# An attention and two-MoE kernel on one core: q and k by block transposes, w_in split on chip, expert weights in 6 KB pieces

## Chip, cores and metric

The program runs on one core of a Trainium2 chip. The metric is the device time of one execution in microseconds, the median of several runs; lower is better. An execution with a profile beside it gives the trace from which all rows below come.

## The reference

Three stages follow each other; everything is float32 at the interface (w_in and w_out arrive as 64-bit floats).

```
attention: q, k, v (4 batches, 12 heads, 448 x 64), causal softmax      -> x (1792 x 768)
MoE 1:     h = x @ w_in (768 x 2048); g = h * clip(h + 3, 0, 6) / 6; x2 = g @ w_out
MoE 2:     logits = x2 @ phi (768 x 32); softmax over tokens -> slot_input = d.T @ x2 (32 x 768)
           per expert e of 8, 4 slots each: relu(slot_input[e] @ w1[e]) @ w2[e]
           out = softmax over slots(logits) @ slot_out                 (1792 x 768)
```

w1 is 8 x 768 x 1024 and w2 8 x 1024 x 768, 25.2 MB each; the output is 5.5 MB.

## The kernel before

**A planner writes the program.** The function records steps (an engine or a choice of engines, a supposed cost, the steps it depends on, the buffers it uses, a priority). `Schedule.run` then picks steps one after the other by its own clock and emits them; each engine executes its instructions in that order. The table `TU` (L20) holds the priorities of the stages, biases and buffer counts. All DMAs are issued from SP, in one order, on one queue of 16 DMA engines; a DMA whose buffer isn't free holds up those behind it.

**Attention** (L408) works on pairs of heads, six pairs per batch, 24 in all. For q and for k of a pair, `ld` (L416) loads both heads to a tile of 112 partitions in pieces of 256 bytes; `tr` (L431) makes four PE transposes into PSUM; ACT copies the result to the rounded half `qp[:,0]` or `kp[:,0]`; DVE subtracts to get the rest, `[:,1]` (L440). Then come the scores for the maxima (L457, DVE L472), the maxima's diagonal (L486 to L490, on POOL or DVE), the scores again, transposed (L507, L512), exp on ACT (L522), the causal cut on POOL (L530), the product with v (L545), normalisation on DVE and a transpose back (L566).

**w_out and w_in** are converted from 64-bit floats once (`conv`, L581: raw load of 768 KB, ACT, three DVE steps). w_out goes to a scratch `wo_d` in DRAM. w_in, in 16 parts `ft` of 128 columns, is split into a rounded half (ACT, L682) and a rest (DVE L685 or POOL L687), in the tile `wpl` of 768 KB. In batch 0 the converted part is stored to `wf_d` (384 KB) and the split pair to `wi_d` (768 KB). Batches 1 and 2 load the split pair straight from `wi_d`. Batch 3 loads the 384 KB from `wf_d` and splits again. There are two `wpl` and two `cx` buffers.

**MoE 1** (`hmm`, L698 to L701) takes 18 matmuls for each `ft`, 64 such groups in all, called H0 to H63 here. Its activation (L706, L708), the transposes of g (L715) and the logits (L730) follow each. Groups of batch b stand between the attention pairs of batch b+1, so that PE has both at hand.

**MoE 2** waits for the whole of MoE 1. It loads w1 as 32 tiles of 768 KB in pieces of 2 KB (L1015), and w2 in three column chunks of 384, 256 and 128 (`DCH`, L881): 16 tiles of 768 KB in pieces of 1.5 KB, 16 of 512 KB in pieces of 1 KB, 8 of 512 KB in pieces of 512 bytes. The tiles, `ring`, become free as earlier stages release memory: twelve of w1 are loaded before H63 ends. Each chunk of w2 ends with a short chain: copy (L1133), a PE sum over row groups (L1138), ACT and DVE (L1140, L1142), 16 products (L1155 and its copies L1164, L1168) and four output DMAs. The first chunk's outputs are issued among the later loads.

## Time and profile before

| What | Value |
|---|---|
| median of 3 runs | 681.69 us (681.17 to 682.29) |
| profiled execution, own time | 680.19 us |
| its span, first to last instruction | 678.4 us |
| PE busy | 628.4 us (93%) |
| DVE, ACT, POOL busy | 329.7, 261.4, 96.5 us |
| DMA | 161.56 MB, 238 GB/s over the span |
| packets | 142615, of which 71632 under 512 B |

The profile counts busy time per engine, cuts the span into slices, follows the chain of waits back from the end, and gives for any stretch the busy time of each engine, the clock granted to PE, and how much of the DMA engines' time was taken. A DMA share slightly over 1 means that packets overlap on an engine.

### The profile page before, as it was taken

What the parts mean: (1) busy time and instruction counts of PE and PEld (TensorE: products, weight loads), DVE (VectorE), ACT (ScalarE), POOL (GpSimd) and SP (SyncE); (2) the same over time, 40 slices, a digit from 0 to 9 for tenths busy, and PEclk for the clock granted to TensorE, in tenths of its full rate; (3) what the DMA queues carried; (4) which work ended last, traced back from release to release, by engine and by line L of the source; (5) the groups of instructions that cost most, each with busy time, mean ns of one, the idle gap of its engine ahead of it and who ended that gap; (6) DMA issues with size and microseconds to landing.
All of it is one profiled execution on the core that took longest, in us unless ns stands there. A gap on an engine that the chain in (4) does not pass through costs nothing.

```text
span 678.4 us, 15815 instructions
## 1 busy us (share of the span) xinstructions
PE 628.4 (93%) x6556; PEld 478.2 (70%) x6556; DVE 329.7 (49%) x814; ACT 261.4 (39%) x488; POOL 96.5 (14%) x197
## 2 busy tenths in 40 slices
PE   8798989999999999999999999999999999977474
PEld 6677868787888778888888688888698843522133
DVE  6886978888784534444335554323433333101101
ACT  2575566544544433323334332334344322201011
POOL 1332332325340011110001001000000000000000
PEclk7998999999999999999999999999999999996666
DMA  8989899989979833555445343335962399999997
GB/s 205 312 293 297 270 262 335 338 236 333 298 267 361 264 89 122 157 159 138 141 142 168 91 135 124 124 135 212 370 239 93 117 341 385 378 373 357 331 313 220
DMA packets 142615, 161.56 MB, mean 238 GB/s; under 512 B 71632, under 2 KB 113872, under 8 KB 142544
## 3 DMA queue, kind: packets, MB, share of 16 engines
q1 hardware_dynamic: 142544, 160.56, 72.9%
q8 instruction: 51, 0.84, 0.5%
q14 instruction: 20, 0.16, 0.1%
HBM read 129.86 MB, written 30.67 MB: 237 GB/s over the span
## 4 chain that ended last, share of the span: by engine, by line
PE 68%; DMA 13%; DVE 9%; SPq 3%; issue 2%; ACT 2%; POOL 0%; DVEq 0%; ACTq 0%; POOLq 0%
PE ph L701 19%; PE pl L701 13%; DMA ring<-in_moe_w_dram 7%; PE ps L507 5%; PE t L715 5%; DVE ps L472 4%; DMA raw<-in_moe_w_out_dram 3%; PE o L545 3%; SPq L401 3%; PE t L566 3%; PE ps L457 2%; PE t L434 2%; PE t L859 2%; PE ps L1025 2%; PE ph L730 2%
## 5 line engine op out<-in xcount | busy, mean ns | idle before, releaser
L701 PE MATMUL ph<-xp,wpl 128*128 128x448 f32 x720 | 157.0, 371 | 0.0
L701 PEld LDWEIGHTS ph<-xp,wpl 128*128 128x128 f32 x720 | 132.2, 188 | 15.2 <-ACT r L706 2.2
L701 PE MATMUL pl<-xp,wpl 128*128 128x448 f32 x432 | 94.2, 371 | 0.0
L701 PEld LDWEIGHTS pl<-xp,wpl 128*128 128x128 f32 x432 | 79.4, 188 | 9.0 <-issue 2.6
L472 DVE CUSTOM_DVE_ANT_0 ps<-ps,maskw 128x448 f32<-128x448 f32 (+3 forms) x144 | 61.7, 429 | 48.5 <-PE ps L457 38.6
L530 POOL TENSOR_SCALAR_AFFINE_SELECT s<-s 128x256 f32<-128x256 f32 x96 | 43.6, 478 | 232.9 <-ACT s L522 141.5
L706 ACT ACTIVATE r<-ph,three 128x448 f32<-128x448 f32 x40 | 25.5, 637 | 102.5 <-PE ph L701 102.5
L507 PE MATMUL ps<-qp,kp 64*64 64x64 f32 (+3 forms) x576 | 57.5, 306 | 3.8 <-ACT s L522 3.8
L522 ACT ACTIVATE s<-ps 128x896 f32<-128x896 f32 (+2 forms) x72 | 50.3, 734 | 25.9 <-PE ps L512 22.0
L708 DVE SCALAR_TENSOR_TENSOR g<-r,ph 128x448 f32<-128x448 f32 x40 | 24.7, 618 | 62.9 <-ACT r L706 62.9
L507 PEld LDWEIGHTS ps<-qp,kp 64*128 64x128 f32 (+1 forms) x576 | 42.1, 175 | 17.7 <-issue 6.6
L545 PE MATMUL o<-vr,s 128*64 128x65 f32 (+1 forms) x1536 | 53.6, 224 | 0.0
L545 PEld LDWEIGHTS o<-vr,s 128*64 128x64 f32 (+1 forms) x1536 | 48.6, 137 | 5.8 <-issue 3.8
L587 ACT ACTIVATE ca<-raw 128x768 f32<-128x768 f32 x32 | 29.3, 917 | 29.7 <-DMA raw<-in_moe_w_out_dram 10.0
L708 DVE SCALAR_TENSOR_TENSOR g<-r,pl 128x448 f32<-128x448 f32 x24 | 14.8, 617 | 50.8 <-ACT r L706 50.8
L720 ACT ACTIVATE gtok<-t 128x384 f32<-128x384 f32 x64 | 31.2, 487 | 19.2 <-PE t L715 19.0
L715 PE MATMUL t<-ident,g 128*128 128x128 f32 (+1 forms) x256 | 37.9, 279 | 0.2 <-DVE g L708 0.2
L706 ACT ACTIVATE r<-pl,three 128x448 f32<-128x448 f32 x24 | 15.3, 636 | 58.3 <-PE pl L701 58.3
L596 DVE SCALAR_TENSOR_TENSOR cw<-ca,cw 128x768 uint32<-128x768 uint32 x32 | 32.9, 1029 | 3.4 <-ACT ca L587 1.7
L1123 PE MATMUL o<-ring,wos 128*32 128x384 f32 (+1 forms) x256 | 22.5, 474 | 11.8 <-DMA ring<-in_moe_w_dram 11.8
L715 PEld LDWEIGHTS t<-ident,g 128*128 128x128 f32 (+1 forms) x256 | 26.9, 133 | 6.1 <-issue 1.5
L457 PE MATMUL ps<-kp,qp 64*128 64x448 f32 (+1 forms) x192 | 27.3, 344 | 4.1 <-DVE mc L472 3.0
(209 smaller groups left out, 827.1 us busy)
## 6 DMA issues: line engine op xcount, KB each, us to landing
ring<-in_moe_w_dram SPq DMA_DIRECT2D x45, 768.0 KB, 11.6
wpl<-wi_d SPq DMA_DIRECT2D x32, 768.0 KB, 4.2
raw<-in_moe_w_out_dram SPq DMA_DIRECT2D x16, 768.0 KB, 6.1
raw<-in_moe_w_in_dram SPq DMA_DIRECT2D x16, 768.0 KB, 7.4
wi_d<-wpl SPq DMA_DIRECT2D x16, 768.0 KB, 6.1
ring<-in_moe_w_dram SPq DMA_DIRECT2D x21, 512.0 KB, 8.0
wo_d<-gtok SPq DMA_DIRECT2D x16, 384.0 KB, 4.1
wf_d<-cx SPq DMA_DIRECT2D x16, 384.0 KB, 7.5
```

The costliest lines, as they stand in the source:

```text
L457: nc.tensor.matmul(ps.t[:n, h, c:c + w], pl["q"].t[r, 0, q0:q0 + n], pl["k"].t[r, 0, 0:w], start=(t == part[0][0]), stop=adds, skip_group_ ...
L472: nc.vector.tensor_tensor_reduce(out=x, in0=x, in1=maskw[:n, 320 - q0:320 + n] if t else maskw[:n, 320:320 + n], scale=-1.0, scalar=3.0e38 ...
L507: nc.tensor.matmul(ps.t[:kn, h, col:col + n], pl["k"].t[r, x, q0:q0 + kn], pl["q"].t[r, y, q0:S], start=(c == 0 and col == 0), stop=False, ...
L522: nc.scalar.activation(out=o, in_=x, func=ACTF.Exp, scale=SCALE)
L530: nc.gpsimd.affine_select(out=x, in_=x, pattern=[[0, 2], [1, kn]], compare_op=ALU.is_ge, fill=0.0, base=0, channel_multiplier=-1)
L545: nc.tensor.matmul(o.t[64 * h:64 * h + 64, VD * j:VD * j + VD], s.t[:kn, h, c:c + 64], vr.t[:kn, h, t, :], start=(t == 0), stop=(t == ts[- ...
L596: e = sc.add("DVE", 1.04, lambda: nc.vector.scalar_tensor_tensor(out=cw.t, in0=ca.t.bitcast(U32), scalar=3, in1=cw.t, op0=ALU.logical_shif ...
L701: nc.tensor.matmul(h.t[:, :S], w.t[:, a, kk, :], x.t[:, c, kk, :], start=(n == 0), stop=(n == len(seq) - 1))
L706: rr = sc.add("ACT", 0.63, lambda h=h, r=r: nc.scalar.activation(out=r.t, in_=h.t[:, :S], func=ACTF.Relu, bias=three), [hh], [h, r], pr - ...
L708: gg = sc.add("DVE", 0.62, lambda h=h, r=r, g=g: nc.vector.scalar_tensor_tensor(out=g.t, in0=r.t, scalar=6.0, in1=h.t[:, :S], op0=ALU.min, ...
L715: nc.tensor.transpose(tp.t[:n, t * P:(t + 1) * P], g.t[:, t0:t0 + n], ident)
L720: nc.scalar.activation(out=gflat[:, :3 * DFF].rearrange("p (t f) -> p t f", f=DFF)[:, :, c], in_=v3[:, 0:3, :], func=ACTF.Copy)
```

## The change

Four things, and a new table of planner numbers.

1. For batches 1 to 3 (pairs 6 to 23, `DV`), q and k are loaded in 32 x 32 blocks, pieces of 128 bytes, four DMAs a tensor instead of two. DVE transposes the blocks in one instruction into an SBUF tile `tt` of which there are two; ACT and DVE (or POOL) split from there.
2. w_in's split is never stored. Batch 0 stores the converted part (384 KB); batches 1 to 3 load it and split it on ACT and DVE or POOL.
3. w1 is read as 32 tiles of 768 KB in contiguous pieces of 6 KB. w2 of experts 0 to 5 likewise (24 tiles, both column halves); w2 of experts 6 and 7 in two column halves (8 tiles, pieces of 1.5 KB). Rows of a weight matrix thus lie on partitions in another order, and two small operands (`sis`, `hs`) are read by PE with a stride to match.
4. The output comes in two column halves of 384 instead of three chunks; all eight output DMAs stand behind the last weight load. Both halves are summed in one PSUM tile.

```diff
-TU = {'PO': [0.0, -20.32, -45.9, 12.37], 'TO': [5.04, -0.39, 13.98, 19.64], 'PB': 0.45, 'AB': 0.24, 'TB': 274.35, 'DUTY': 0.6, 'RINGS': [2, 4, 2, 3, 1, 6, 2, 3], 'LOOK': 0.44, 'FILL': 0.96, 'RAW': 3, 'CA': 1, 'CW': 1, 'S': 2, 'PAIR': 15.98, 'UNIT': 2.62, 'WP0': 17.76, 'WPS': 10.66, 'T0': 138.06, 'L0': 10.86, 'L1': 6.43, 'GP': 217.47, 'TP': 6.75, 'ZP': 84.29, 'UP': -2.56, 'P0': 12.1, 'NQ': 2, 'WAIT': 0.12, 'AHEAD': 2.2, 'LAT': 0.23, 'CX': 2, 'G': 5, 'R': 1, 'VR': 2, 'XT': 2, 'Q': 1, 'AS': 1.42, 'A1': -2.92, 'A2': 3.39, 'A3': 17.95, 'A4': 12.3, 'A5': 8.23, 'A6': 23.03, 'A7': 6.65, 'DG': 2, 'DA': 6}
+TU = {'PO': [0.0, -14.01, -18.7, -2.86], 'TO': [-7.42, -5.8, 41.18, 1.8], 'PB': 0.71, 'AB': -0.57, 'TB': 242.38, 'DUTY': 0.6, 'RINGS': [2, 4, 2, 3, 1, 6, 2, 3], 'LOOK': 0.28, 'FILL': 0.96, 'RAW': 3, 'CA': 1, 'CW': 1, 'S': 2, 'PAIR': 11.35, 'UNIT': 2.56, 'WP0': 31.11, 'WPS': 9.72, 'T0': 166.71, 'L0': 16.88, 'L1': 5.94, 'GP': 249.05, 'TP': 9.64, 'ZP': 104.14, 'UP': -2.06, 'P0': 15.72, 'NQ': 2, 'WAIT': 0.11, 'AHEAD': 2.19, 'LAT': 0.23, 'CX': 2, 'G': 5, 'R': 1, 'VR': 2, 'XT': 2, 'Q': 1, 'AS': 1.42, 'A1': -4.01, 'A2': 3.42, 'A3': 15.93, 'A4': -9.99, 'A5': 12.02, 'A6': 20.26, 'A7': 9.91, 'DG': 2, 'DV': 6, 'TT': 2, 'LO': 1.0, 'DA': 6}
...
+                    for c in range(2 * blocks):
+                        r = 64 * h + 32 * c
+                        dma(buf.t[r:r + 32, :S].rearrange("p (n d) -> p n d", d=32),
+                            src[b, 2 * hp + h, :, 32 * c:32 * c + 32].rearrange("(n p) d -> p n d", p=32))
...
+                if blocks:
+                    a = sc.add("DVE", 0.62, lambda tp=tp, buf=buf: nc.vector.transpose(tp.t, buf.t[:, :S]), [l], [tp, buf, dst], p0)
+                else:
+                    a = sc.add("PE", 0.5, tr, [l], [tp, buf, dst], p0)
...
+                lo = [("DVE", 0.61, lambda tp=tp, dst=dst: nc.vector.tensor_sub(
+                    dst.t[:, 1], tp.t[:, :S], dst.t[:, 0].bitcast(F32)))]
+                if blocks:
+                    lo.append(("POOL", 1.2, lambda tp=tp, dst=dst: nc.gpsimd.tensor_sub(
+                        dst.t[:, 1], tp.t, dst.t[:, 0].bitcast(F32))))
...
-                if b == 0:
-                    wi_stored[ft] = sc.load(
-                        0.79e6, lambda w=w, ft=ft: dma(wi_d[ft], w.t.bitcast(F32)), [wr], [w], ps_)
-                elif not fin:
-                    wr = sc.load(0.79e6, lambda w=w, ft=ft: dma(w.t.bitcast(F32), wi_d[ft]), [wi_stored[ft]], [w], ps_ - 10)
+                    wi_stored[ft] = sc.load(0.39e6, lambda cx=cx, ft=ft: dma(wi_d[ft], cx.t), [cr], [cx], ps_)
+                else:
+                    cr = sc.load(0.39e6, lambda cx=cx, ft=ft: dma(cx.t, wi_d[ft]), [wi_stored[ft]], [cx], ps_ - 10)
...
-        DCH = [(0, 384), (384, 256), (640, 128)]
+        DCH = [(0, DM // 2), (DM // 2, DM // 2)]
...
-                    dma(w.t.rearrange("p (k f) -> p k f", k=3),
-                        w1[e, kh * 384:(kh + 1) * 384, f * 512:(f + 1) * 512].rearrange("(k p) f -> p k f", p=P))
+                    dma(w.t, w1[e, kh * 384:(kh + 1) * 384].rearrange("(p k) f -> p (k f)", p=P)[:, g * RING:(g + 1) * RING])
...
+        for e in range(SPLIT):
+            for k0 in range(0, 8, 2):
+                l = w2load(e, k0, 2, 0, 2, 0)
+        for ci in range(2):
+            for e in range(SPLIT, E):
+                for k0 in (0, 4):
+                    l = w2load(e, k0, 4, ci, 1, ci)
+        obs = [[sc.buf("ring" if ci else "osb") for _ in range(B)] for ci in range(2)]
...
-            sc.load(1792.0 * n, fn, ev + ([l] if ci else []), [ob], T1 + 900 + 100 * ci)
+            sc.load(1792.0 * n, fn, ev + [l], [ob], T1 + 900 + 100 * ci)
```

PE in the middle of the program, before: from the product with v of one pair (L545) to the group H21 (L701) and the scores behind it. Names: `qr`, `kr` are the loaded q and k, `ident` the identity, `xp` the input of MoE 1.

```order
L545 MATMUL o_248<-vr_217,s_225 64x65 x32
L457 MATMUL ps_247<-kp_224,qp_222 128x192 x2
L457 MATMUL ps_247<-kp_224,qp_222 128x320 x2
L434 MATMUL t_249<-ident,qr_215 128x112 x4
L434 MATMUL t_250<-ident,kr_216 128x112 x4
L701 MATMUL ph_244<-xp_196,wpl_198 128x448 x18
L566 MATMUL t_249<-ident,xt_233 64x64 x14
L507 MATMUL ps_247<-qp_222,kp_224 128x448 x6
L512 MATMUL ps_247<-dg_232,oner 128x448 x2
```

The same place in the change (line numbers are those of the changed kernel: L559 is the product with v, L708 the group):

```order
L559 MATMUL o_234<-vr_203,s_211 64x65 x32
L471 MATMUL ps_233<-kp_210,qp_208 128x192 x2
L471 MATMUL ps_233<-kp_210,qp_208 128x320 x2
L722 MATMUL t_235<-ident,g_176 128x128 x3
L722 MATMUL t_235<-ident,g_176 64x128
L708 MATMUL ph_231<-xp_180,wpl_182 128x448 x18
L521 MATMUL ps_233<-qp_208,kp_210 128x448 x6
L526 MATMUL ps_233<-dg_218,oner 128x448 x2
L521 MATMUL ps_233<-qp_208,kp_210 64x64 x6
```

The two rows of four transposes are gone; a transpose of g stands there now. In all, 144 of 192 PE transposes of q and k go.

DVE of the change where a pair of batch 3 is prepared:

```order
L444 STREAM_TRANSPOSE tt_201<-qr_199 128x448
L444 STREAM_TRANSPOSE tt_202<-kr_200 128x448
L450 TENSOR_TENSOR qp_207<-tt_201,qp_207 128x448
L450 TENSOR_TENSOR kp_209<-tt_202,kp_209 128x448
L486 ISA ps_233,mc_214<-ps_233,maskw 128x448
L486 ISA mc_214 128x1
```

The two block transposes stand together, then the two rests, which wait for ACT's copies. Between the first and the sixteenth activation product of MoE 1 (L708, now L715), DVE had 13 rests of q and k, 9 splits of w_in, 1 diagonal and 11 first steps of `conv`; now 12 block transposes, 6 rests, 3 splits, 3 diagonals and 12 such steps stand there. In the whole program POOL's splits go from 7 to 31, and 10 rests of q and k move to it.

SP at the end, before (`ring` tiles hold weights or outputs):

```order
L401 DMA ring_5952<-in_moe_w_dram 128x8x128
L401 DMA out_dram<-ring_6126 112x4x256
L401 DMA out_dram<-ring_6130 112x4x256
L401 DMA out_dram<-wos 112x4x256
L401 DMA out_dram<-ring_6134 112x4x256
L401 DMA out_dram<-ring_107 112x4x128
L401 DMA out_dram<-ring_111 112x4x128
L401 DMA out_dram<-wos 112x4x128 x2
```

and in the change:

```order
L401 DMA ring_5391<-in_moe_w_dram 128x4x384
L401 DMA ring_5395<-in_moe_w_dram 128x4x384
L401 DMA out_dram<-wos 112x4x384 x4
L401 DMA out_dram<-ring_5933 112x4x384
L401 DMA out_dram<-ring_5937 112x4x384
L401 DMA out_dram<-ring_5941 112x4x384
```

Four outputs from `wos` (the first half) and four from `ring` now follow the last weights. The first half has two buffers for four outputs (`osb`), as before.

DVE at the same place in the change:

```order
L1178 COPY wos<-ps_233 112x384
L1178 COPY wos<-ph_231 112x384
L1178 COPY wos<-ps_233 112x384 x2
L1146 COPY wos<-o_234 64x384
L1178 COPY wos<-ps_233 112x384 x2
L1156 SCALAR_TENSOR_TENSOR sl<-sh,flag,t_235 128x384
L1178 COPY ring_5933<-ph_231 112x384
```

L1178 copies products to the output buffers, L1146 takes the sums of a half: the second half's copy (L1146) and its L1156 stand behind copies of the first half's third and fourth output.

## Rows read from the trace of the kernel before

**Rows 1.** The page: busy us of each engine, and GB/s moved in 40 equal slices.
```profile
PE 628.4 (93%) x6556; PEld 478.2 (70%) x6556; DVE 329.7 (49%) x814; ACT 261.4 (39%) x488; POOL 96.5 (14%) x197
...
GB/s 205 312 293 297 270 262 335 338 236 333 298 267 361 264 89 122 157 159 138 141 142 168 91 135 124 124 135 212 370 239 93 117 341 385 378 373 357 331 313 220
```

**Rows 2.** Windows: busy us of PE, PEld, DVE, ACT, POOL (count), clock, DMA share, GB/s.
```profile
0.00:107.40 107.40, 94.73 (x1362) 75.79 (x1362) 84.93 (x162) 61.61 (x97) 32.52 (x64) 0.95 0.90 277
107.40:229.90 122.50, 120.61 (x1252) 100.37 (x1248) 91.29 (x205) 64.01 (x115) 36.20 (x56) 1.00 0.93 308
229.90:542.60 312.70, 310.34 (x2876) 256.55 (x2874) 128.25 (x365) 114.35 (x231) 25.96 (x76) 1.00 0.48 154
543.50:678.40 134.90, 101.78 (x1073) 45.05 (x1071) 25.07 (x84) 20.79 (x45) 1.80 (x1) 0.82 1.03 339
```

**Rows 3.** Chain of waits, whole span: start us, us, what.
```profile
107.47 3.84 PE ph L701 x18
...
332.84 0.92 PE t L434 x8
...
538.77 3.84 PE ph L701 x18
```

**Rows 4.** Chain of waits, the last 60 us.
```profile
621.82 1.26 PE t L1138 x2
623.10 0.50 ACT sh L1140
623.62 0.62 DVE sl L1142
...
626.40 4.97 DMA out_dram<-wos
...
643.40 23.36 DMA ring<-in_moe_w_dram x3
...
666.81 1.01 PE o L1123 x16
```

**Rows 5.** Groups of instructions with shapes kept apart: xcount, busy us, mean ns, idle before.
```profile
L682 ACT ACTIVATE wpl<-cx 128x768 fp32r<-128x768 f32 x32 | 26.9, 841 | 2.1 <-DVE cx L599 1.9
...
L685 DVE TENSOR_TENSOR wpl<-cx,wpl 128x768 fp32r<-128x768 f32 x25 | 24.3, 970 | 10.1 <-ACT wpl L682 9.5
...
L440 DVE TENSOR_TENSOR qp<-t,qp 128x448 fp32r<-128x448 f32 x24 | 14.9, 620 | 20.3 <-ACT qp L404 20.2
...
L687 POOL TENSOR_TENSOR wpl<-cx,wpl 128x768 fp32r<-128x768 f32 x7 | 13.5, 1925 | 15.9 <-ACT wpl L682 15.9
...
L1164 DVE COPY wos<-ps 112x384 f32<-112x384 f32 x6 | 3.1, 552 | 3.4 <-PE ps L1155 3.4
```

**Rows 6.** What the DMA queue's own engine, SP, waited for: total us, times, longest.
```profile
SPq L401 <- DVE wpl L685: 72.0, 19, 8.8
```

**Rows 7.** DMA issues: line, engine, xcount, KB each, median us to landing.
```profile
wpl<-wi_d SPq DMA_DIRECT2D x32, 768.0 KB, 4.2
...
out_dram<-wos SPq DMA_DIRECT2D x4, 672.0 KB, 5.6
...
phis<-in_moe_phi_dram SPq DMA_DIRECT2D x1, 96.0 KB, 2.3
```

**Rows 8.** Windows in which pieces of one size fill the queue; columns as in 2.
```profile
192.20:194.20 2.00, 2.00 (x14) 1.82 (x13) 1.86 (x3) 0.13 (x1) 0.66 (x1) 1.00 1.00 413
471.00:476.00 5.00, 5.00 (x30) 3.82 (x29) 2.21 (x3) 1.97 (x5) 0.00 (x0) 1.00 1.03 413
555.00:583.00 28.00, 26.63 (x265) 11.49 (x261) 7.70 (x38) 4.68 (x11) 1.80 (x1) 1.00 1.05 386
593.00:609.00 16.00, 11.96 (x172) 5.17 (x168) 1.68 (x5) 1.69 (x3) 0.00 (x0) 1.00 1.06 372
...
1.50:5.00 3.50, 3.50 (x18) 2.54 (x16) 3.09 (x23) 0.58 (x1) 0.30 (x2) 1.00 0.77 174
5.90:6.60 0.70, 0.40 (x4) 0.16 (x4) 0.60 (x2) 0.49 (x1) 0.00 (x0) 1.00 0.91 149
```

More of the change, by code (lines that the diff above doesn't have):

```diff
@@ L303 @@
         wo_d = [dram.tile([P, DM], F32, name=f"wo_d{i}") for i in range(KF)]
-        wf_d = [dram.tile([P, KD, P], F32, name=f"wf_d{i}") for i in range(KF)]
-        wi_d = [dram.tile([P, 2, KD, P], F32, name=f"wi_d{i}") for i in range(KF)]
+        wi_d = [dram.tile([P, KD, P], F32, name=f"wi_d{i}") for i in range(KF)]
         sc = Schedule()
@@ L986 @@
         sp = []
[L987 to L996 removed]
+        si_ev = [
+            sc.add("DVE", 0.3, lambda: nc.vector.tensor_copy(held["sis"][:, :192], si.t[:, 0, :192]), [oe], [si], T1),
+            sc.add("ACT", 0.26, lambda: nc.scalar.activation(
+                out=held["sis"][:, 192:], in_=si.t[:, 0, 192:384], func=ACTF.Copy), [oe], [si], T1),
+        ]
+        for c in range(3):
+            sp.append(sc.add("PE", 0.12, lambda c=c: nc.tensor.matmul(
+                sp3.t[:, c * 64:(c + 1) * 64], held["sis"][:, c::3],
+                selb.rearrange("p d s -> p (d s)"), start=True, stop=True), si_ev + [rr, he], [sp3], T1))
         sit = sc.add("DVE", 0.3, lambda: nc.vector.tensor_copy(
@@ L1095 @@
                 op0=ALU.mult, op1=ALU.subtract), [a], [tp], pr + b))
+        SPLIT = E - 2
         parts = []
[L1099 to L1111 removed]
@@ L1112, with w2half, w2load, ld @@
-        obs = [[sc.buf("ring" if ci else "osb") for _ in range(B)] for ci in range(3)]
+        def w2half(e, kh):
+            return w2[e, kh * 512:(kh + 1) * 512].rearrange("(p k) d -> p k d", p=P)
+        def w2load(e, k0, kn, c0, cn, ci):
+            w = sc.buf("ring")
+            w.k = [(k0 + k, c, (k * cn + c - c0) * 384) for k in range(kn) for c in range(c0, c0 + cn)]
+            def ld(e=e, w=w):
+                dma(w.t.rearrange("p (k d) -> p k d", k=kn),
+                    w2half(e, k0 // 4)[:, k0 % 4:k0 % 4 + kn, c0 * 384:(c0 + cn) * 384])
+            l = sc.load(0.72e6 if cn > 1 else 0.76e6, ld, [], [w], T1 + 1000 + 100 * ci + e)
+            parts.append((e, w, l, ci))
+            return l
@@ L1131 @@
             pr = T1 + 900 + 100 * ci
-            ss = lambda n=n: held["ss"][:, :n]
-            a = sc.add("DVE", 0.07 + n * 1.04e-3, lambda ps=ps, n=n: nc.vector.tensor_copy(
-                held["ss"][:, :n], ps.t[:, :n]), [a, oe] + sdone, [ps], pr)
-            if ci == 2:
+            half = slice(64 * ci, 64 * ci + 64)
+            a = sc.add("DVE", 0.07 + n * 1.04e-3, lambda half=half, n=n: nc.vector.tensor_copy(
+                held["ss"][half, :n], yacc.t[half, :n]), [ylast, oe] + sdone, [yacc], pr)
@@ L1136 @@
+            if ci == 1:
                 sc.add("SP", 0.0, fill_on, [a], [], 0)
             so = sc.buf("t")
-            a = sc.add("PE", n * 1.2e-3, lambda so=so, n=n: nc.tensor.matmul(
-                so.t[:, :n], sel4.rearrange("p a s -> p (a s)"), held["ss"][:, :n], start=True, stop=True), [a], [so], pr)
+            a = sc.add("PE", n * 1.2e-3, lambda so=so, n=n, half=half, ci=ci: nc.tensor.matmul(
+                so.t[:, :n], sel4[half].rearrange("p a s -> p (a s)"), held["ss"][half, :n],
+                start=True, stop=True, tile_position=(64 * ci, 0)), [a], [so], pr)
```

97 lines of the change are left out of this document (35 added, 62 removed).

## Prediction

> **What bounds the kernel now.** I read the page's busy times first [rows 1], then the windows by stage [rows 2], then the chain of waits for the places where the stages meet [rows 3, 4], and at last the groups, waits and DMA rows that price the change. On the page the reader is to see that PE is busy for 93% of the span, and that the GB/s stand at 89 to 168 through most of the middle and at 313 to 385 in the last stage, but for the last slice. The windows say why. From 0 to 107.4 us (attention of batch 0, conversion of w_out) PE is busy for 94.7 us, DVE for 84.9, and the DMA share is 0.90: three things are near their limit. From 107.4, where the first group of MoE 1 starts [rows 3], to 229.9, PE is idle for 1.9 us of 122.5; DVE is busy for 91.3 and the DMA share is 0.93. From 229.9 to 542.6 PE is idle for 2.4 us of 312.7, and everything else is at half load or less. From 543.5 on, after the last group of MoE 1 has ended (538.77 + 3.84), the DMA share is 1.03 to the end: the weights of MoE 2 decide. The chain there runs over DMA loads for long pieces, 23.4 us of it from 643.4 on; the last weights release PE at 666.8, and 11.6 us later the kernel ends [rows 4].
>
> So there are two paths, PE up to 542.6 and DMA after it, and the change touches both. I work the sum out against the profiled execution: 680.19 us, of which 678.4 are the span. The median of the runs, 681.69, is 1.5 us above it; I add that at the end. A measurement of this kernel can tell about 0.2% (1.4 us) from no change.
>
> **Middle: what goes.** 144 of the 192 PE transposes of q and k go, eight per pair for 18 pairs. Eight take 0.92 us [rows 3]: 18 x 0.92 = 16.6 us on an engine that idles for 4.3 us in 435 [rows 2]. This comes off the path in full if nothing else gets late.
>
> **Middle: what is added, and where it hides.** The 36 block transposes on DVE have no row. Nearest is a DVE subtraction of the same 128 x 448, 0.62 us; scaled from the one that reads no PSUM, 0.97 x 448/768 = 0.57; the far end is POOL's rate for such a plane, 1.93 x 448/768 = 1.12 [rows 5]. I take 0.62: 22.3 us in all (20 to 40). Between 107.4 and 229.9 the order puts 12 of them in (7.4 us) and takes out 7 rests at 0.62 and 6 splits at 0.97 (10.2 us), which go to POOL; two diagonals and a conversion step come in, some 3 us. DVE stays at 91.5 of then 117 us. After 229.9 it gets 18 transposes (11.2), 14 splits (13.6) and five diagonals (about 7), less two rests: 128 becomes 159 of some 302 us. ACT gets 32 more splits at 0.84, 27 us, POOL 24 more at 1.93 and ten rests at 1.12, 57 us, less six diagonals; both have far more idle time than that [rows 2]. If DVE's cover were gone, the next thing late would be the maxima's reductions, and PE's second scores behind them.
>
> The split pair used to arrive by a load of 768 KB that lands 4.2 us after its issue, and could be issued only when its buffer was free [rows 7]. Now half as much is loaded ahead into `cx`, and after the buffer is free only ACT (0.84) and DVE (0.97) or POOL (1.93) stand between, 1.8 to 2.8 us, while the other buffer feeds a group of 3.8 us [rows 3, 5]. This wait gets shorter, not longer. The 16 stores of the split, for which SP alone waited 72.0 us [rows 6], go as well; q and k cost SP 72 more issues, and I cost these at nothing, since the waiting that leaves SP covers them. If it did not, the loads of v and of `cx` behind them would come late.
>
> The DMA engines: the stores are 12.6 MB, at 413 GB/s 30.5 us of queue time [rows 8]. Against that stand the pieces of 128 bytes. A window full of 256-byte pieces moved 174 GB/s at share 0.77, which is 226 at share 1; the one of 128-byte pieces, phi's, 149 at 0.91, or 164 [rows 8]. A pair's q and k are 459 KB: 2.03 us before, 2.80 now. For seven pairs in the stretch this adds 5.4 us, and 113.9 us of DMA work become 89 of 117. So the queue is relieved. I deduct 2 us for new waits in DVE's order, where the two rests stand behind ACT's copies. The first 107 us I leave as they are. **Middle: 14.6 us less** (7 to 19).
>
> **Last stage.** 52 tiles of 786 KB, 40.9 MB, are still to come after 543.5, before as after. In the change 44 are read in 6 KB pieces and 8 in 1.5 KB pieces. No read of 6 KB pieces fills the queue in this trace. Pieces of 2 KB from the same tensors gave 386 GB/s, reads of 3 KB pieces, with a few of 2 KB, 413, and 6 KB stores also 413 [rows 8]; I take 400 (386 to 413). That is 34.6 MB / 400 = 86.5 us, and 6.3 MB at the 372 of 1.5 KB pieces, 16.9 us; with 1.5 us to start, the last weights land at 543.5 + 104.9 = 648.4 instead of 666.8. Part of these 18.4 us is only moved: the first output chunk of 2.75 MB went among the loads, and now follows them.
>
> After the last weights the end is longer. The first half has two buffers for four outputs. Outputs 1 and 2 queue behind the weights (1.85 us each at 372); the first has landed after some 1.9 + 2.0 us, when the copy of the third may start, as a copy waited 4.97 us for such a landing before [rows 4]. Two copies in a row on DVE, 0.55 each [rows 5], then the second half's chain, which in DVE's order stands behind them: copy 0.55, PE sum 1.26, ACT 0.50, DVE 0.62 [rows 4], held up by the fourth output's copies for about another 1. That makes 9. Sixteen products follow, copied at 0.55 by two engines, 4.4 us, and the last output, 672 KB, lands about 5 us after its issue [rows 7]. Sum 18 us instead of 11.6, 6.4 lost. **Last stage: 18.4 - 6.4 = 12.0 us less** (8.9 at 386 GB/s, 14.7 at 413).
>
> **Sum.** 680.2 - 14.6 - 12.0 = 653.6 for a profiled execution, 655 for the median.
>
> **Rivals.** *The pieces gain little.* If what binds is not the piece but the memory behind it, 6 KB reads run at the 372 of 1.5 KB pieces: 93.0 us instead of 86.5, the last stage gains 5.5, and the median is 661.6. For it speaks that from 1.5 to 2 KB the rate rises by only 4%; against it the 413 with 3 KB pieces [rows 8]. The Trainium skill (DMA: Bandwidth & Descriptors, "Where 436 GB/s comes from") says that about 358 GB/s per core bind for transfers between HBM and SBUF. At that rate the estimate for these tiles would be 96.6 us. The trace does not agree: 386 and 413 stand there.
>
> *The freed PE time fills with waits.* Then DVE or POOL sets the pace of a pair: in order, DVE transposes q and k, waits for ACT twice, and only then reaches the reductions. At 0.8 us per pair 14.4 of the 16.6 us are given back: the middle gains 2, and the median is 668. For it: DVE at 0.75 to 0.79 of the first two stretches; against it: no more DVE work there than before, and PE works a pair ahead.
>
> *More than forecast.* In the first 107.4 us PE idles for 12.7 [rows 2]. If the new order and fewer transposes in it give back half of that, the median is 649.
>
> *Slower than before.* The mechanism would be the pieces of 128 bytes on the one DMA queue between 107.4 and 229.9. There 28 us of room are left by the sum above, 4 us per pair; it decides from 6.8 us for a pair's 459 KB, 2.4 times the time that phi's pieces took. To give back the whole 26.6 us as well, a pair would have to take 10.6 us (43 GB/s), and the median would pass 682. The Trainium skill (DMA: Bandwidth & Descriptors, Specifications) puts the least transfer at line rate at 512 bytes and says that below it the engine reads, modifies and writes. That the rate falls with small pieces the trace shows; a fall to 43 GB/s it does not, 164 being measured, though on one load of 96 KB only.
>
> *The change does not do what it says* in one way: if the early order is so much worse that the first stretch grows by what the rest gains. Nothing in the rows says so; it shares the chance of the slower case.
>
> **Chances.** Forecast 0.55; the pieces gain little 0.17; waits 0.13; more than forecast 0.10; slower 0.05, of which 0.01 within 0.2%. The first four are all faster by over 0.2%: 0.95 faster, 0.01 same, 0.04 slower. The bounds of the two terms reach from 680.2 - 19 - 14.7 + 1.5 = 648 to 680.2 - 7 - 5.5 + 1.5 = 669. I set the range at 645 to 668: it takes in the better case and most of that with waits, and leaves out the slower one.
>
> **What the profile of the change would show.** If the middle is right, the last group of MoE 1 ends at 526 to 530 instead of 542.6, PE's idle time between first and last group stays under 8 us, the block transposes take near 0.62 us, and DMA's share between 107 and 230 falls under 0.8. If the last stage is right, GB/s stand near 400 for some 85 us, the last weights land about 105 us after the end of the last group, and a gap in the DMA share comes between the second and third output. The forecast is wrong where the rate of 6 KB pieces stays at or below 386, where PE waits for splits or maxima, or where the end after the last weights is not near 18 us.

## The result, and the profile of the changed kernel

The median is 660.71 us (659.93 to 664.11) against 681.97 (681.17 to 682.29) before: a ratio of 0.970, with a 95% interval from 0.9664 to 0.9735. The forecast was 655, in a range from 645 to 668. So the sign and the range held, and the forecast promised 5.7 us too much.

The page of the changed kernel, busy times and GB/s in 40 slices, answers to [rows 1]:

```profile
PE 618.7 (94%) x6288; PEld 471.9 (72%) x6288; DVE 375.3 (57%) x882; ACT 281.6 (43%) x516; POOL 151.9 (23%) x201
...
GB/s 196 252 305 280 216 257 235 190 211 230 233 214 177 246 162 68 94 113 85 95 75 115 91 68 87 49 53 248 378 240 65 121 264 367 417 415 414 395 305 247
```

PE lost 9.7 us, DVE gained 45.6, POOL 55.4, and the last stage moves 414 to 417 GB/s where 357 to 385 stood. The windows, with the columns of [rows 2], show where the time went; MoE 1 starts at 111.6 here and ends at 533.7, and at 640.5 PE starts on the last weights (they had landed at 637.9; see the account of the last stage):

```profile
0.00:111.60 111.60, 94.16 (x1356) 74.79 (x1356) 87.23 (x160) 59.39 (x95) 40.65 (x73) 0.95 0.84 245
111.60:230.30 118.70, 115.40 (x1196) 94.80 (x1193) 99.90 (x216) 66.85 (x118) 57.49 (x58) 1.00 0.79 218
230.30:533.70 303.40, 302.93 (x2798) 249.16 (x2797) 161.19 (x422) 134.81 (x262) 51.99 (x69) 1.00 0.42 123
533.70:555.00 21.30, 18.97 (x246) 9.79 (x245) 6.74 (x25) 4.49 (x12) 1.80 (x1) 0.92 0.91 349
555.00:617.00 62.00, 60.09 (x560) 32.55 (x560) 9.40 (x41) 7.50 (x15) 0.00 (x0) 0.92 1.02 414
617.00:640.50 23.50, 16.79 (x94) 5.33 (x94) 3.66 (x7) 2.73 (x6) 0.00 (x0) 1.00 0.99 349
640.50:659.30 18.80, 10.32 (x49) 5.52 (x48) 7.23 (x14) 5.84 (x13) 0.00 (x0) 0.82 0.75 237
```

The span shrank by 678.4 - 659.3 = 19.1 us. The stretch up to the first group of MoE 1 grew by 4.2; from there to the end of the last group it is 422.1 instead of 435.2, 13.1 less; the last stage takes 125.6 instead of 135.8, 10.2 less.

The first border has to be read with care. In the new order the second half of the transposed scores of pair 6, 1.2 us of PE, stands ahead of H0 and not behind it. And the stretch ahead of H0 scatters: in three runs with one and the same order up to there it took 109.7, 111.6 and 113.3 us (experiments 4 and 8 are the other two), in two runs of the old order 107.4 and 110.6 (experiment 2), the longer one with a mean granted clock of 0.91 instead of 0.95. The end of the last group is the better mark: 530.7, 533.7 and 534.9 us in the new order, 542.6 and 546.1 in the old. By the means the middle, with all that lies ahead of it, is 11.3 us shorter. With 10.2 for the last stage that makes 21.5; the medians differ by 21.3.

### The profile page after: what moved, and what is told of

Read it like the earlier page. It is cut to its first block, busy times and chain, and to the rows that moved or that the text cites. A ratio compares the mean times of both kernels' runs of the same rounds, so it can differ in the third digit from the quotient of the medians.

```text
span 659.3 us, 15417 instructions
## 1 busy us (share of the span) xinstructions
PE 618.7 (94%) x6288; PEld 471.9 (72%) x6288; DVE 375.3 (57%) x882; ACT 281.6 (43%) x516; POOL 151.9 (23%) x201
## 4 chain that ended last, share of the span: by engine, by line
PE 69%; DMA 11%; DVE 8%; SPq 3%; ACT 3%; issue 3%; POOL 1%; DVEq 0%; ACTq 0%; POOLq 0%
PE ph L708 22%; PE pl L708 10%; PE ps L521 5%; PE o L559 5%; DMA raw<-in_moe_w_out_dram 4%; PE t L722 4%; DMA ring<-in_moe_w_dram 4%; SPq L401 3%; PE t L580 3%; PE ps L471 2%; DVE ps L486 2%; PE t L1045 2%; PE ph L1030 2%; PE t L866 2%; PE ps L1030 2%
## 5 line engine op out<-in xcount | busy, mean ns | idle before, releaser
L708 PE MATMUL ph<-xp,wpl 128*128 128x448 f32 x828 | 180.7, 371 | 1.5 <-POOL wpl L699 1.1
L708 PEld LDWEIGHTS ph<-xp,wpl 128*128 128x128 f32 x828 | 152.1, 188 | 19.5 <-ACT r L713 2.9
L544 POOL TENSOR_SCALAR_AFFINE_SELECT s<-s 128x256 f32<-128x256 f32 x96 | 51.5, 559 | 153.1 <-ACT s L536 143.5
L699 POOL TENSOR_TENSOR wpl<-cx,wpl 128x768 fp32r<-128x768 f32 x31 | 60.5, 1951 | 86.0 <-ACT wpl L694 80.9
L486 DVE CUSTOM_DVE_ANT_0 ps<-ps,maskw 128x448 f32<-128x448 f32 (+3 forms) x144 | 61.7, 429 | 19.1 <-PE ps L471 15.3
L708 PE MATMUL pl<-xp,wpl 128*128 128x448 f32 x324 | 71.3, 373 | 0.0
L715 DVE SCALAR_TENSOR_TENSOR g<-r,ph 128x448 f32<-128x448 f32 x46 | 28.4, 617 | 65.6 <-ACT r L713 62.1
L708 PEld LDWEIGHTS pl<-xp,wpl 128*128 128x128 f32 x324 | 59.6, 188 | 6.4 <-issue 1.1
L694 ACT ACTIVATE wpl<-cx 128x768 fp32r<-128x768 f32 x64 | 53.6, 838 | 13.6 <-PE ph L708 6.0
L521 PEld LDWEIGHTS ps<-qp,kp 64*128 64x128 f32 (+1 forms) x576 | 41.6, 174 | 24.2 <-issue 9.4
L559 PE MATMUL o<-vr,s 128*64 128x65 f32 (+1 forms) x1536 | 53.6, 224 | 0.0
L559 PEld LDWEIGHTS o<-vr,s 128*64 128x64 f32 (+1 forms) x1536 | 48.6, 137 | 5.6 <-issue 3.7
L697 DVE TENSOR_TENSOR wpl<-cx,wpl 128x768 fp32r<-128x768 f32 x33 | 31.6, 958 | 17.1 <-ACT wpl L694 15.2
L1137 PE MATMUL o<-ring,wos 128*32 128x384 f32 x232 | 27.3, 502 | 5.3 <-DMA ring<-in_moe_w_dram 5.3
```

What stands on the lines that cost most here:

```text
L486: nc.vector.tensor_tensor_reduce(out=x, in0=x, in1=maskw[:n, 320 - q0:320 + n] if t else maskw[:n, 320:320 + n], scale=-1.0, scalar=3.0e38 ...
L521: nc.tensor.matmul(ps.t[:kn, h, col:col + n], pl["k"].t[r, x, q0:q0 + kn], pl["q"].t[r, y, q0:S], start=(c == 0 and col == 0), stop=False, ...
L544: nc.gpsimd.affine_select(out=x, in_=x, pattern=[[0, 2], [1, kn]], compare_op=ALU.is_ge, fill=0.0, base=0, channel_multiplier=-1)
L559: nc.tensor.matmul(o.t[64 * h:64 * h + 64, VD * j:VD * j + VD], s.t[:kn, h, c:c + 64], vr.t[:kn, h, t, :], start=(t == 0), stop=(t == ts[- ...
L694: e = sc.add("ACT", 0.84, lambda w=w, cx=cx: nc.scalar.activation(out=w.t[:, 0], in_=cx.t, func=ACTF.Copy), [cr], [cx, w], ps_)
L697: ("DVE", 1.0, lambda w=w, cx=cx: nc.vector.tensor_sub(w.t[:, 1], cx.t, w.t[:, 0].bitcast(F32))),
```

## The experiments

Eleven kernels ran, in groups, each group with the kernel before on its chip; where the order of work matters, I say whether the planner kept it. The times from H0 to the end of the last group come from windows in each trace.

### 1. q and k on PE again

```diff
-'DV': 6
+'DV': 24
```

> The changed kernel, but q and k of all 24 pairs are transposed on PE as before. Theory (PE's own time is what the middle is made of): the 144 transposes come back on PE's path, 18 x 0.92 = 16.6 us less the some 3 us that PE's other work grew by, so the last group of MoE 1 ends near 547 us instead of 533.7 and the kernel takes 672 to 678 us. Rival (waits on DVE and POOL took most of the freed time): the group ends at 537 to 542 and the kernel takes 664 to 669 us, with less idle time of PE than the changed kernel has.

Measured: 668.67 us (667.65 to 669.16), ratio 0.978; the last group ends at 541.2. By the time it is the rival's case. But PE's idle time tells more. The window from H0 to the end of the last group, first of this kernel, then of the changed one:

```profile
108.09:541.21 433.12, 431.86 (x4145) 358.00 (x4144) 245.13 (x609) 200.12 (x380) 78.86 (x124) 1.00 0.47 143
```
```profile
111.58:533.70 422.12, 418.36 (x3992) 343.98 (x3989) 261.10 (x637) 201.69 (x379) 109.49 (x127) 1.00 0.53 150
```

With PE's transposes the engine idles for 1.3 us, with DVE's for 3.8, and ahead of H0 for 14.5 against 17.4. The 16 pairs whose transposes lie in this window save 11.0 us, or 9.8 if the 1.2 us of pair 6's scores are counted in, where 16 x 0.92 would have been 14.7. Part of that is the size of the term: on the timeline of the kernel before, four transposes mostly start 0.3 to 0.55 us ahead of what follows them, 13.4 us for the 16 pairs, or 0.84 per pair and 15.1 for 18. The rest is mostly waiting: PE idles 2.5 us longer in this window. Experiments 6 and 9 say where.

### 2. The last part alone, on the kernel before

The column chunks, the loads of w1 and w2, the strided small operands and the outputs are the changed kernel's; all else, and the planner's table, is the kernel before.

```diff
-DCH = [(0, 384), (384, 256), (640, 128)]
+DCH = [(0, DM // 2), (DM // 2, DM // 2)]
...
```

> The kernel before with the last part of the change alone: expert weights in 6 KB pieces, outputs in halves. Theory (the last stage is a sum of bytes over a rate and an end chain, whatever came ahead of it): the last group of MoE 1 ends at 540 to 544 us as before, the last stage takes 124 to 127 us as in the changed kernel, and the median is 670 to 674 us. Rival (the last stage gained because buffers came free in another order in the changed kernel): the last stage takes 129 us or more and the median is over 675 us.

Measured: 672.41 us (670.09 to 673.28), ratio 0.983. The last group ends at 546.1, later than expected because the first stretch took 110.6; from H0 to the end of the last group it is 435.5 us, as before (435.2). The last stage takes 124.2. So the theory holds: this stage is a sum of bytes over a rate and an end chain, whatever came ahead.

### 3. w_in split once and stored, as before

```diff
-wi_stored[ft] = sc.load(0.39e6, lambda cx=cx, ft=ft: dma(wi_d[ft], cx.t), [cr], [cx], ps_)
+wi_stored[ft] = sc.load(0.79e6, lambda w=w, ft=ft: dma(wi_d[ft], w.t.bitcast(F32)), [wr], [w], ps_)
...
-cr = sc.load(0.39e6, lambda cx=cx, ft=ft: dma(cx.t, wi_d[ft]), [wi_stored[ft]], [cx], ps_ - 10)
+wr = sc.load(0.79e6, lambda w=w, ft=ft: dma(w.t.bitcast(F32), wi_d[ft]), [wi_stored[ft]], [w], ps_ - 10)
```

> The changed kernel, but w_in is split once, in batch 0, and the split pair stored and loaded by all three later batches: 6.3 MB more stores and 18.9 MB more loads. Theory (PE sets the middle and the DMA queue has room there): the DMA share from the first group of MoE 1 on for some 120 us rises from 0.79 to above 0.9, and the median stays within 3 us of the changed kernel, 658 to 664 us. Rival (the relief of the DMA queue and of SP is what the gain rests on): PE waits for the pair or for q and k, and the median is 667 to 675 us.

Measured: 671.23 us (668.32 to 673.26), ratio 0.981: the rival's range. The DMA share behind H0 rose to 0.85 only, not above 0.9. From H0 to the start of the 17th group, and from there to the end of the last:

```profile
110.97:231.09 120.12, 114.01 (x1189) 94.30 (x1185) 96.09 (x207) 65.02 (x114) 52.78 (x64) 1.00 0.85 259
231.09:541.99 310.90, 308.76 (x2827) 251.70 (x2828) 131.06 (x392) 103.07 (x218) 21.47 (x54) 1.00 0.59 184
```

That is 431.0 us, 8.9 more than in the changed kernel, 4.5 of them idle time of PE and 4.4 work. The planner made another order here and put in more filler matmuls (matmuls whose result nobody reads, L385; 136 instead of 112 up to the end of MoE 1). And only 1.9 of the 8.9 us lie up to the 17th group (118.3 us in the changed kernel), though the last store has landed by then, at 226.0; the other 7.0 lie behind it, where the larger loads are. In another order this mark is rough, but the run does not say by itself that the stores are the cause. Experiment 5 keeps the order.

### 4. The small operand read without a stride

```diff
-out=held["hs"], in_=hp.t, func=ACTF.Copy), [a, oe]
+out=held["hs"].rearrange("p (i c) -> p i c", i=4),
+in_=hp.t.rearrange("p (c i) -> p i c", i=4), func=ACTF.Copy), [a, oe]
...
-held["hs"][:, i::4]
+held["hs"][:, i * P:(i + 1) * P]
```

> The changed kernel, but the copy of the first expert product writes it out in the order in which PE loads it, so that PE's weight load reads neighbouring elements instead of every fourth. Theory (DMA sets the last stage, 415 GB/s through it): the four small products per expert fall from 1.96 to about 1.0 us, 8 us of PE time in all, and the median moves by no more than 1 us (659.5 to 661.5). Rival (PE's slower small products hold the ring of weight tiles back): the median falls by 4 to 8 us, to 653 to 657.

Measured: 662.18 us (656.86 to 665.83), ratio 0.967. Groups of instructions in the last stage, the changed kernel and this one (count, busy us, mean ns):

```profile
L1045 PE MATMUL t<-sele,wos 128*128 128x8 f32 x64 | 16.3, 380 | 1.6 <-ACT wos L1040 1.6
L1045 PEld LDWEIGHTS t<-sele,wos 128*128 128x128 f32 x64 | 15.5, 327 | 8.4 <-issue 5.0 <-ACT wos L1040 3.4
```
```profile
L1046 PE MATMUL t<-sele,wos 128*128 128x8 f32 x64 | 8.5, 259 | 1.6 <-ACT wos L1040 1.6
L1046 PEld LDWEIGHTS t<-sele,wos 128*128 128x128 f32 x64 | 7.7, 191 | 7.7 <-issue 4.2 <-ACT wos L1040 3.4
```

The stride costs 7.8 us of PE, which the prediction had not seen at all, and not one of them shows: the last stage takes 124.9 us instead of 125.6. So PE's own time does not set it, as the theory has it.

### 5. The split pairs stored for nobody, in the same order

```diff
+ws_d = [dram.tile([P, 2, KD, P], F32, name=f"ws_d{i}") for i in range(KF)]
...
+def sub(eng, w=w, cx=cx, b=b, ft=ft):
+    eng.tensor_sub(w.t[:, 1], cx.t, w.t[:, 0].bitcast(F32))
+    if b == 0:
+        dma(ws_d[ft], w.t.bitcast(F32))
```

> The changed kernel in the same order on every compute engine, but each of batch 0's 16 split pairs is also stored to DRAM and read by nobody: 12.6 MB more on the DMA queue, SP waiting for each split, and the pair's buffer held until the store has ended. Theory (these stores were a cost of the kernel before, on the path through the conversion of w_in): the last group of MoE 1 ends 4 to 9 us later than in the changed kernel, and the median is 664 to 670 us. Rival (the run with the stored split was slow only since its order of work and its fillers were others): 2 us later at most, median 659 to 663 us.

Measured: 683.72 us (681.39 to 689.60), ratio 1.005 (1.002 to 1.009). The whole gain is gone; it cost 23 us, far over what the theory gave. From H0 to the start of the 16th group, the changed kernel and this one, and then one of DVE's waits in this one:

```profile
111.58:219.98 108.40, 105.69 (x1103) 87.32 (x1100) 93.68 (x198) 61.02 (x107) 56.85 (x56) 1.00 0.79 215
```
```profile
110.40:233.12 122.72, 111.24 (x1103) 91.37 (x1100) 93.08 (x198) 61.54 (x107) 54.05 (x56) 0.94 0.89 278
```
```profile
DVE cx L614 <- DMA wi_d<-cx: 14.1, 5, 4.4
```

14.3 us of the loss lie in this stretch: 8.8 are idle time of PE, and in the other 5.5 the same matmuls run longer, at a mean granted clock of 0.94 instead of 1.00. The next group adds 7.0 us, where the splits wait 7.5 us for a load of `cx` in the same queue. The same instructions run; what is new is that the last conversion step waits five times, 14.1 us in all, for the store of the converted part, which now stands behind the pair's store in the one queue and frees `cx` late. Everything that DVE has to do behind it waits too. In the changed kernel the same wait is 0.3 us (its group's row stands in experiment 11). The order had not been planned for these stores, so 23 us need not be what they cost the kernel before. That kernel shows the same wait in the same stretch, 6.7 us (its row stands in the next part). With the stores back, the gain of the middle is gone here and mostly gone in experiment 3 (431.0 us from H0 to the end of the last group, 435.2 before the change).

### 6. Every block transpose twice, in the same order

```diff
-lambda tp=tp, buf=buf: nc.vector.transpose(tp.t, buf.t[:, :S])
+tb
...
+def tb(tp=tp, buf=buf):
+    for _ in range(2):
+        nc.vector.transpose(tp.t, buf.t[:, :S])
```

> The changed kernel in the same order, but each block transpose of q and k is done twice into the same tile: 36 x 0.62 = 22.3 us more on DVE, 7.4 of it in the stretch where MoE 1 of batch 0 meets the conversion of w_in and DVE is busy for 0.86 of the time. Theory (DVE has become a limit of that stretch and covers nothing more there, while later it has room): 4 to 9 us longer, median 665 to 670 us, all of it before the 16th group of MoE 1. Rival (DVE hides it as forecast): under 2 us, median 659 to 663 us. If PE waited for every pair: 15 us or more, median over 675 us.

Measured: 665.98 us (662.51 to 669.46), ratio 0.977. From H0 to the start of the 16th group, and from there to the end of the last:

```profile
111.45:224.68 113.23, 107.34 (x1103) 88.46 (x1100) 100.09 (x210) 61.77 (x107) 52.93 (x56) 0.98 0.74 198
224.68:537.91 313.23, 312.50 (x2892) 256.91 (x2890) 177.67 (x460) 141.73 (x273) 49.89 (x71) 1.00 0.43 128
```

The first of these is 4.8 us longer than in the changed kernel, the second as long (313.7 there), though more extra transposes fall into it. Of the 4.8 us, 3.2 are idle time of PE and 1.6 the same matmuls at a granted clock of 0.98 instead of 1.00. The theory holds in the main: beside the conversion of w_in DVE covers only a third of the 7.4 us, later it covers all of it.

### 7. The planner's old constants

```diff
-TU = {'PO': [0.0, -14.01, -18.7, -2.86], ...
+TU = {'PO': [0.0, -20.32, -45.9, 12.37], ... 'DV': 6, 'TT': 2, 'LO': 1.0}
```

> The changed kernel with the planner's constants of the kernel before, only the three new ones added. Theory (the first stretch grew by 4 us through the order that the new constants make): the first group of MoE 1 starts near 107 us again and the median is 655 to 659 us. Rival (the constants fit the new work, and what the first stretch loses comes back later): the group starts near 107 us, PE idles more behind it, and the median is 663 us or more. Third possibility: the start of that group moves by the granted clock alone, as two runs in one order differ by up to 3 us, and the median stays within 659 to 663 us.

Measured: 662.09 us (659.38 to 663.87), ratio 0.970. H0 starts at 107.5, but the last group ends at 534.1, where it ended before the constants were put back. So the start is as theory and rival had it, and the time that of the third case: what the first stretch grew by was mostly a border that moved, not time lost, and the table itself is worth nothing that can be measured here.

### 8. Four buffers for the first half's outputs

```diff
-sc.buf("ring" if ci else "osb") for _ in range(B)
+sc.buf("ring" if ci or b > 1 else "osb") for b in range(B)
...
-sc.load(1792.0 * n, fn, ev + [l], [ob], T1 + 900 + 100 * ci)
+sc.load(1792.0 * n, fn, ev + ([l] if ci else []), [ob], T1 + 900 + 100 * ci)
```

> The changed kernel, but the third and fourth output of the first half get ring tiles as buffers, so that no copy waits for an output to land, and the first half's outputs no longer wait for the last weights. Theory (the gap in the DMA share between the second and third output is time lost): DMA share stays near 1 between 635 and 650 us, the kernel ends 14 to 16 us after the last weights instead of 18.8, and the median is 656 to 659 us. Rival (the second half's own chain of sum, two planes and sixteen products sets the end): 18 to 19 us after the last weights, median 660 to 663 us.

Measured: 661.78 us (659.03 to 663.62), ratio 0.971. A window of this kernel around the outputs, the changed kernel's first:

```profile
635.00:650.00 15.00, 12.90 (x66) 6.45 (x62) 7.09 (x14) 5.58 (x12) 0.00 (x0) 1.00 0.75 239
```
```profile
635.00:650.00 15.00, 11.09 (x48) 5.27 (x48) 6.97 (x14) 6.75 (x15) 0.00 (x0) 1.00 0.81 248
```

The share between 635 and 650 rose only from 0.75 to 0.81: the second half's sum, planes and products leave the queue gaps of their own. And the end did not become shorter. The 18.8 us of the expectation count from PE's start on the last weights; from there it is 18.2 us here (639.1 to 657.3). From the landing of the last weights (635.5 here) it is 21.8 us, 21.5 in the changed kernel. The last stage takes 126.6 us instead of 125.6. So the time is the rival's. The last output is issued sooner after that landing, 15.2 us instead of 16.6, but takes 5.8 us to land instead of 4.0, as the outputs of the second half now follow each other closer.

### 9. Block transposes for batches 2 and 3 only

```diff
-'DV': 6
+'DV': 12
```

> The changed kernel, but block transposes only for batches 2 and 3; batch 1's q and k, whose pairs fall into the stretch where w_in is converted, are transposed on PE as those of batch 0. Theory (a block transpose pays where DVE has room, and costs as much as it saves where DVE is at its limit): up to the 16th group of MoE 1 the time is that of the run with all transposes on PE, some 213 us instead of 220, and behind it that of the changed kernel, some 314 us instead of 328; the last group ends at 527 to 530 us and the median is 653 to 657 us. Rival (DVE's limit is not what PE waited for; six pairs' transposes are simply put back on PE, 6 x 0.84 = 5 us): the last group ends at 537 to 541 us and the median is 664 to 668 us. Between: a wash, 659 to 662 us.

Measured: 661.16 us (655.94 to 663.64), ratio 0.966: the case between, a wash. From H0 to the end of the last group:

```profile
111.86:534.99 423.13, 421.85 (x4043) 348.11 (x4042) 257.06 (x637) 200.96 (x380) 97.79 (x120) 1.00 0.51 146
```

Up to pair 12 the order on PE is that of experiment 1, and there 433.1 us stood. So the twelve pairs of batches 2 and 3 give 10.0 us, 0.83 per pair: all that their transposes took. The six pairs of batch 1 give nothing that can be measured, where 5 us were to be had: the last group ends at 535.0 here (531.9 in experiment 10) and at 530.7 to 534.9 with them, while PE idles for 1.3 us from H0 to that end here and for 3.1 to 3.8 with them. My theory had added a first part from one order to a second part from another; the 16th group stands at another place in them, and so the sum was too good.

### 10. The same with four output buffers and the small operand in order

The edits of 4, 8 and 9 together.

> The same with four buffers for the four outputs of the first half, which no longer wait for the last weights, and with the first expert product copied out in the order in which PE loads it. Theory (the end after the last weights becomes 1.5 to 2 us shorter, as in the run with four buffers alone, and the rest adds nothing): 651 to 656 us. Rival (what the outputs gain at the end is taken from the weights in the same queue): the same time as the run with block transposes in batches 2 and 3 alone, within 1 us.

Measured: 662.76 us (659.66 to 663.77), ratio 0.969 (0.966 to 0.973). From the landing of the last weights (634.8) to the end it is 23.2 us, no shorter than without the buffers (22.9 in experiment 9). The theory's range is missed; no version run here beats the changed kernel by what can be measured.

### 11. No subtraction of two tensors on POOL

```diff
-("POOL", 2.0, lambda w=w, cx=cx: nc.gpsimd.tensor_sub(
-    w.t[:, 1], cx.t, w.t[:, 0].bitcast(F32))),
...
-if blocks:
-    lo.append(("POOL", 1.2, lambda tp=tp, dst=dst: nc.gpsimd.tensor_sub(
-        dst.t[:, 1], tp.t, dst.t[:, 0].bitcast(F32))))
```

> The changed kernel, but POOL takes none of the subtractions of two tensors: the second half of each w_in pair (31 of them on POOL in the changed kernel) and the rests of q and k (10) are all DVE's. Theory (POOL's subtractions lengthen DVE's steps that read two tensors of SBUF, so POOL takes little off DVE in the stretch where DVE is at its limit): the conversion steps there fall from 1.27 and 1.36 us to 1.0 to 1.1, DVE's busy share between the first and the 16th group of MoE 1 stays within 0.05 of the changed kernel's 0.86, and the median within 2 us of it, 659 to 663 us. Rival (POOL's help is worth its count: some 16 splits and 5 rests of that stretch go back to DVE, 18 us): DVE passes 0.95 there, PE waits, and the median is 667 us or more.

Measured: 669.95 us (666.89 to 673.47), ratio 0.982. Groups on DVE between 108 and 225 us, the changed kernel, experiment 1, and this one; the first of a pair is the last conversion step, the second the one ahead of it:

```profile
L613 DVE SCALAR_TENSOR_TENSOR cx<-raw,cw 128x768 uint32<-128x768 uint32 x15 | 20.4, 1359 | 0.8 <-POOL s L544 0.4 <-DMA wi_d<-cx 0.3
L610 DVE SCALAR_TENSOR_TENSOR cw<-ca,cw 128x768 uint32<-128x768 uint32 x15 | 19.0, 1268 | 1.1
```
```profile
L613 DVE SCALAR_TENSOR_TENSOR cx<-raw,cw 128x768 uint32<-128x768 uint32 x14 | 14.3, 1019 | 2.6 <-POOL wpl L699 1.2 <-DMA wi_d<-cx 1.1
L610 DVE SCALAR_TENSOR_TENSOR cw<-ca,cw 128x768 uint32<-128x768 uint32 x13 | 13.7, 1054 | 1.0 <-ACT ca L601 0.2
```
```profile
L610 DVE SCALAR_TENSOR_TENSOR cx<-raw,cw 128x768 uint32<-128x768 uint32 x16 | 17.2, 1078 | 0.3
L607 DVE SCALAR_TENSOR_TENSOR cw<-ca,cw 128x768 uint32<-128x768 uint32 x16 | 17.2, 1074 | 0.5
```

The rests of q and k, from the same tile as in the changed kernel (min, median and max ns; there the median was 818 and 819):

```profile
L450 DVE TENSOR_TENSOR qp<-tt,qp x18: 610/625/826, 83.4 to 423.4; 128x448 fp32r<-128x448 f32 x18
L450 DVE TENSOR_TENSOR kp<-tt,kp x18: 609/618/819, 84.0 to 423.9; 128x448 fp32r<-128x448 f32 x18
```

The theory is right on the steps, 1.27 and 1.36 us became 1.07 and 1.08, and on DVE's share (92.2 of 105.1 us, 0.88). The rests say that it is POOL's subtractions and not the source in SBUF that made them longer. It is wrong on the time. H0 starts at 119.2, PE's work ahead of it is 103.6 us instead of 94.2, partly fillers (148 up to the end of MoE 1 instead of 112, 24.2 us of PE instead of 18.8), and the last group ends 9.5 us later. The planner, with all the subtractions on DVE, put H0 later. As this planner plans it, POOL's help is worth its contention; what it is worth in one and the same order is not shown.

## Why the prediction was right, and where it was not

**First stretch, left as it is.** Nothing that can be measured: experiment 7 puts H0 back at 107.5 and the end does not move.

**Middle, 14.6 less.** Measured 11.3 by the ends of the last group. The step that failed is "DVE stays at 91.5 of then 117 us", that is, that DVE hides the block transposes of batch 1. The transposes cost what I took: the tile's instructions on the changed kernel (min, median and max ns) are

```profile
L444 DVE STREAM_TRANSPOSE tt<-qr x18: 631/636/647, 77.8 to 400.4; 128x448 f32<-128x448 f32 x18
L444 DVE STREAM_TRANSPOSE tt<-kr x18: 595/603/605, 78.3 to 401.0; 128x448 f32<-128x448 f32 x18
...
L450 DVE TENSOR_TENSOR kp<-tt,kp x14: 611/819/1228, 114.7 to 402.9; 128x448 fp32r<-128x448 f32 x14
L450 DVE TENSOR_TENSOR qp<-tt,qp x12: 618/818/1008, 82.7 to 402.0; 128x448 fp32r<-128x448 f32 x12
```

But DVE was busy for 99.9 of 118.7 us there, not for 91.5. I had counted what leaves DVE for POOL (splits and rests) and not what POOL's work then does to the steps that stay. The rests, now from SBUF beside POOL's work, take 0.82 us instead of 0.62 [rows 5], and 0.62 again where POOL subtracts nothing (experiment 11). The conversion steps take 1.27 and 1.36 us (their rows stand in experiment 11); in the kernel before, between 107.4 and 229.9, they took 1.07 and 0.98:

```profile
L596 DVE SCALAR_TENSOR_TENSOR cw<-ca,cw 128x768 uint32<-128x768 uint32 x13 | 13.9, 1068 | 0.8
L599 DVE SCALAR_TENSOR_TENSOR cx<-raw,cw 128x768 uint32<-128x768 uint32 x14 | 13.7, 981 | 8.0 <-DMA wf_d<-cx 6.7 <-POOL wpl L687 1.2
```

DVE at its limit delays the maxima and the pieces of MoE 1; six of the eighteen pairs gave nothing that can be measured (experiment 9), 7.4 us more of transposes there cost 4.8 (experiment 6). So the rival of the filled-up time was right for one pair in three, at its 0.8 us per pair, and wrong for the others. The other mis-sized term is small: a pair's eight transposes are 0.84 us of PE's time, not 0.92. Together: 12 pairs at 0.83 make 10.0 instead of 16.6 - 2.

**The stores, costed at no time of their own.** The prediction had the queue relieved and gave that no place in the sum. The second row above shows what that left out: the last conversion step waited 6.7 us for the store of `cx`, in the changed kernel 0.3. In the changed kernel's order the stores cost 23 us (experiment 5); in an order planned with them, and with larger loads in the later batches, the middle is 8.9 us longer (experiment 3). Block transposes and table without the split on chip end the last group at 542.0, the split on chip and table without block transposes at 541.2, both together at 533.7: the two parts give more together than each alone. Why is not shown. The stores and the transposes of batch 1 press on the same stretch, the one through the queue, the other through DVE; but the pairs that pay in experiment 9 come behind the stores, and so does most of the loss of experiment 3.

**SP's issues, costed at nothing.** Right in the price and wrong in the reason. The 72.0 us of [rows 6] are not the stores' alone. Up to 235 us, where the stores are, and behind it, where the waits are those of batch 3's loads into `cx` and of one load of weights, the kernel before has

```profile
SPq L401 <- DVE wpl L685: 13.1, 5, 4.1
```
```profile
SPq L401 <- DVE wpl L685: 58.9, 14, 8.8
```

So 13.1 us were the stores'. And this waiting did not leave SP; it grew from 72.0 us to

```profile
SPq L401 <- DVE wpl L697: 124.2, 28, 7.6
```

since each load of `cx` now stands behind the split that frees its buffer. It holds nobody up: PE idles for 0.5 us of the 303.4 from the 17th group on.

**The pieces of 128 bytes.** A window in which q and k of a pair arrive, beside one load of `cx`:

```profile
306.50:311.00 4.50, 4.50 (x76) 3.87 (x74) 2.76 (x8) 2.66 (x5) 1.11 (x3) 1.00 0.71 115
```

115 GB/s at a share of 0.71 is 162 at share 1, as forecast (164). DMA share behind H0 fell to 0.79. The slower rival had its place right, the one queue beside the conversion, and not its cause: experiment 5 shows that this place can take back the whole gain.

**Last stage, 12.0 less.** Measured 10.2. The 6 KB pieces ran at 414 GB/s, over the 400 taken, so the rival of pieces that gain little is out; the 1.5 KB pieces at 374 (372 taken). The last weights, issued at 625.74, land 12.1 us later, at 637.9, but PE starts on them only at 640.52. The last DMA issue of weights, and PE around it:

```profile
ring<-in_moe_w_dram SPq DMA_DIRECT2D x1, 768.0 KB, 12.1
```
```profile
638.38 0.43 PE L1169 MATMUL ps<-sl,cT 128*112 128x384 f32 x1 [0.44 <-DVE wos L1178]
638.75 1.49 PE L1137 MATMUL o<-ring,wos 128*32 128x384 f32 x8
640.16 0.43 PE L1169 MATMUL ps<-sl,cT 128*112 128x384 f32 x1
640.52 1.48 PE L1137 MATMUL o<-ring,wos 128*32 128x384 f32 x8
```

In PE's order products of the first half (L1169) stand ahead of the last weights (L1137), and no wait for a DMA is left there. So the weights land 104.2 us after the last group, near the forecast (about 105): the faster pieces gained 3 us, and the start, costed at 1.5 us, took some of it back, where the row from 533.7 to 555 shows 349 GB/s at a share of 0.91.

What was mis-sized is the end. From the landing to the end it is 21.5 us, where 18 were forecast, against 11.6 before. The first part of it, up to the second half's products, took 8.0 us (9 forecast), the last output 4.9 (5 forecast), and the sixteen products with their copies, from 645.9 to 654.4, 8.5 instead of 4.4. The chain of waits shows why:

```profile
649.62 0.45 PE ps L1169
...
650.09 0.57 DVE ring L1178
...
650.71 0.44 PE ps L1169
```

A product and its copy take turns at one PSUM tile, some 1.06 us for both, and two tiles serve the sixteen: 8 x 1.06 = 8.5. The forecast counted the copies alone. ACT's and DVE's copies of the third output waited 2.5 and 1.9 us for the first outputs to land, as foretold. By these marks the stage gained 20.0 us up to the landing (18.4 forecast) and lost 9.9 behind it (6.4 forecast); the two errors partly cancel, and that 10.2 came as near to 12.0 as it did is luck.

## What to carry to other kernels

Work taken off the bounding engine is worth its full time only where the engine that receives it has room; ask stage by stage, since the same step paid 0.83 us per pair in one stretch and nothing in another. When work is spread over two engines, cost also what the second one does to the first one's steps. And before a store that "only fills the queue" is costed at nothing, look what buffer it holds: here a queue at 0.89 of its time set the pace, since a conversion step behind it waited for that buffer. And count an end from the landing of the last load, not from when PE gets to it, with a product and its copy priced together where they share a buffer.
